# Units 0 to 3 of a sparse attention on two score buffers, ahead of a mixture-style pair of MLPs

## The chip, the cores and the metric

The kernel runs on one core of a Trainium2 chip. The metric is the device time of one execution in microseconds (us): the median of three runs. A profile of one further execution was taken by the hardware profiler, and all rows below come from it.

The engines are named as the profile names them: PE is TensorE (PEld its weight loads), DVE is VectorE, ACT is ScalarE, POOL is GpSimd, and SP is SyncE, which here only issues DMAs. "SPq" is SP's queue of such issues.

## The reference

What is computed is an attention with a sparse mask, then two MLPs on its output:

```python
# q, k, v: batch 4, heads 8, sequence 576, head size 64
scores = scale * q @ k^T          # heads 0-3: local mask, 32 back
scores = where(mask, scores, -1e9)   # heads 4-7: strided mask, every 32nd position
attn = exp(scores - max); attn = attn / (sum(attn) + 1e-9)
x = (attn @ v), laid out as 2304 tokens x 512
gate = sigmoid(x @ w_gate); val = x @ w_val          # 512 -> 1536
x = (gate * val) @ w_out                             # 1536 -> 512
h = x @ w_in; g = softplus(h); return g @ w_out2     # 512 -> 2048 -> 512
```

All in float32. On PE every float32 product of the MLPs is done as three passes with high and low parts (`mm3`, lines 71 to 74: high times high, high times low, low times high), so each weight and each activation exists as a pair, `h` and `l`.

## The kernel before, in words

**Attention.** The 8 heads of a batch are four pairs, and a pair of one batch is a *unit*: 16 units, numbered batch by batch. In each batch the first two units are local (heads 0 to 3) and the last two strided. So units 0 to 3 are batch 0, and their outputs are the first 576 tokens of `x`, each unit one of the four 128-row parts that the MLPs sum over.

A unit goes through these steps, each a function: `load` (q and k by DMA, two transfers) and `load_v` (v, two transfers); `bias` (two matmuls that put the mask into PSUM); `scores` (PE, then on DVE a maximum L1048 and a subtraction L1049 into an SBUF tile `sl` or `ss`); `exponent` (ACT L1056); `normalize` (DVE: a sum L1063 and a reciprocal L1066; POOL: the product L1069); `p_transposes` (PE L1090, then copies `pt` by ACT L1094); `values` (PE L1107 into `ps_o`); `outputs` (ACT writes the high part `xh` L1132, DVE the low part `xl` L1135).

**Weights.** They come as 64-bit words, in pieces of 512 KB (`raw`, three buffers, loaded by `load_next` L104), and are decoded in two steps per piece (`decode_steps`): DVE L122 and L126 give `f`, ACT L150 writes the high half, DVE L132 and L139 give `e`, POOL L152 and L153 write the low half. `f` and `e` have one buffer each during the attention. In the kernel before, L122 and L132 write into a PSUM bank (`ps_x`).

**Order.** Nothing is scheduled by a tool: each engine executes its instructions in the order in which the Python code emits them. `first()` emits units 0 to 3 and the first steps of unit 4, written out by hand, and then yields to the MLP, whose matmuls (`window`, `step`, `gates`) fill PE from there on between the steps of units 4 to 15. All loads are on SP's queue in the order of the code, except k of units 0 and 1, which ACT issues. A load into a tile whose last reader isn't done makes SP wait, and everything behind it on SP.

**Buffers.** PSUM has eight banks: `ps_s` (scores, two banks, one tile), `ps_o` (two banks, one tile), `ps_hy` (three banks; transposes of units 0 to 3, warming matmuls, MLP) and `ps_x` (one, decode). q, k and v have three tiles each; `pt` has one.

**Warming.** `keep_busy(n)` emits n matmuls on constants that nothing reads (`ps_w`, L965): six at the start and single ones in `first()`.

**The gate.** `gates(..., interleave=True)` for the first MLP block alternates the two halves of the gate weights (piece 0 and piece 1) over each part of `x`. The result of both is held back until `release()`.

The lines of `first()` that the prediction speaks of, shortened:

```python
bias(0); scores(0); ...; normalize(0); bias(1); scores(1); load_v(2); load(3)
next(decs[0])                      # L122, L126 of piece 0
p_transposes(0); normalize(1); next(decs[0])
bias(2); scores(2); values(0); load(4); load_v(3); outputs(0)
... values(3); outputs(3); bias(4); scores(4); ...
```

## Time and profile before

| | |
|---|---|
| three runs | 883.06, 885.71, 886.19 us; median 885.71 us |
| the profiled execution | 887.23 us, of which 885.4 us is the span from the first to the last instruction |
| mean granted TensorE clock | 0.992 |
| PE busy | 865.7 us, 98% of the span, 6010 matmuls |
| DVE, POOL, ACT busy | 598.2, 490.2, 420.6 us |
| read from HBM, written | 113.75 MB, 38.27 MB |

The profile's page lists busy time by engine, then the span in 40 slices of 22.1 us each with a digit for the busy tenths, then queues, the chain that ended last, and the costliest groups of instructions. A matmul's end is modelled, so PE's busy time says only that PE had work; the start times are what is measured. An idle stretch is put down to what ended it; "issue" means that no semaphore explains it.

### The profile page before, as it was taken

The page shows a single profiled execution, that of the slowest core. Times are in us where ns is not written, and L with a number is a line of the kernel's source. Part 1 is how long each engine was busy: PE and PEld are TensorE (multiplying, and loading weights), DVE is VectorE, ACT ScalarE, POOL GpSimd, SP SyncE. Part 2 cuts the span into 40 slices and gives each one's busy share as a digit, 9 for nine tenths or more (in the row PEclk, how much of TensorE's full clock was granted, in tenths as well). Part 3 has the DMA queues.
Part 4 walks back from the last instruction along what each step waited for, and adds up shares of the span by engine and source line. Part 5 has one row for each costly group of instructions (what it writes and reads, how often), then busy time and mean ns, then how long its engine had stood idle before and what let it go on. Part 6 is the DMA issues. An engine that isn't in the chain of part 4 may idle for free.

```text
span 885.4 us, 15378 instructions
## 1 busy us (share of the span) xinstructions
PE 865.7 (98%) x6010; PEld 725.0 (82%) x6010; DVE 598.2 (68%) x898; ACT 420.6 (48%) x680; POOL 490.2 (55%) x389
## 2 busy tenths in 40 slices
PE   7799999999999999999999999999999999999998
PEld 5578878888888888888888888888888878888887
DVE  6696776268878888878874645665756574656574
ACT  2366544423333333233333466666667575665641
POOL 5373321037888687788778625466536963343630
PEclk9699999999999999999999999999999999999999
DMA  9696460034675577566644245566575565545403
GB/s 276 179 247 163 122 161 4 1 105 134 241 257 191 190 254 233 180 214 231 223 164 165 72 145 181 192 198 196 195 233 183 192 219 183 187 148 182 151 1 118
DMA packets 61367, 153.01 MB, mean 173 GB/s; under 512 B 6160, under 2 KB 6672, under 8 KB 61296
## 3 DMA queue, kind: packets, MB, share of 16 engines
q1 hardware_dynamic: 61008, 151.42, 53.3%
q8 instruction: 47, 0.77, 0.4%
q10 hardware_dynamic: 288, 0.62, 0.2%
q14 instruction: 24, 0.20, 0.1%
HBM read 113.75 MB, written 38.27 MB: 172 GB/s over the span
## 4 chain that ended last, share of the span: by engine, by line
PE 68%; DVE 4%; ACT 3%; POOL 3%; issue 1%; DVEq 0%; POOLq 0%; ACTq 0%
PE ps_y L72 9%; PE ps_y L73 9%; PE ps_y L74 9%; PE ps_v L72 4%; PE ps_v L74 4%; PE ps_v L73 4%; PE ps_g L72 4%; PE ps_g L74 4%; PE ps_g L73 4%; PE ps_h L74 3%; PE ps_h L73 3%; PE ps_h L72 3%; PE ps_b L72 2%; PE ps_b L73 2%; PE ps_b L74 2%
## 5 line engine op out<-in xcount | busy, mean ns | idle before, releaser
L330 POOL TENSOR_TENSOR b<-b,b 128x512 f32<-128x512 f32 (+1 forms) x42 | 72.5, 1739 | 91.7 <-DVE gl L330 46.1
L241 ACT ACTIVATE gh<-ps_v 128x512 fp32r<-128x512 f32 (+1 forms) x60 | 33.3, 555 | 131.5 <-DVE ps_v L284 131.5
L304 DVE TENSOR_TENSOR acc<-ps_y,acc 128x512 f32<-128x512 f32 (+1 forms) x100 | 62.2, 634 | 48.0 <-PE ps_y L74 47.6
L333 ACT ACTIVATE gh<-b 128x1024 fp32r<-128x1024 f32 (+1 forms) x63 | 57.8, 917 | 40.7 <-DVE b L713 23.9
L469 DVE TENSOR_TENSOR acc<-ps_y,acc 128x512 f32<-128x512 f32 x66 | 44.8, 686 | 41.7 <-PE ps_y L74 40.7
L330 POOL TENSOR_TENSOR gl<-b,gh 128x1024 fp32r<-128x1024 f32 x20 | 49.2, 2458 | 36.5 <-ACT gh L333 36.5
L242 DVE TENSOR_TENSOR gl<-ps_v,gh 128x512 fp32r<-128x512 f32 (+1 forms) x60 | 38.3, 638 | 37.5 <-ACT gh L241 37.5
L189 POOL TENSOR_TENSOR a<-f,e 128x512 f32<-128x512 f32 x32 | 41.4, 1295 | 39.6 <-DVE e L139 39.6
L177 POOL TENSOR_TENSOR pair<-a,pair 128x512 fp32r<-128x512 f32 x32 | 41.5, 1298 | 31.7 <-ACT pair L176 31.7
L330 DVE TENSOR_TENSOR gl<-b,gh 128x1024 fp32r<-128x1024 f32 (+1 forms) x43 | 48.7, 1134 | 14.5 <-ACT gh L333 14.3
L74 PE MATMUL ps_y<-gh,w02l 128*128 128x512 f32 (+1 forms) x144 | 53.8, 374 | 0.4 <-POOL w02l L153 0.4
L72 PE MATMUL ps_y<-gh,w12h 128*128 128x512 f32 (+1 forms) x144 | 54.1, 376 | 0.1
L73 PE MATMUL ps_y<-gl,w12h 128*128 128x512 f32 (+1 forms) x144 | 53.7, 373 | 0.0
L126 DVE SCALAR_TENSOR_TENSOR f<-raw,ps_x 128x512 uint32<-128x512 uint32 x68 | 46.8, 688 | 9.4 <-POOL w11l L153 2.1
L284 DVE TENSOR_TENSOR ps_v<-ps_v,sg 128x512 f32<-128x512 f32 (+1 forms) x60 | 38.5, 641 | 21.2 <-PE ps_v L74 20.0
L74 PE MATMUL ps_y<-gh,w12l 128*128 128x512 f32 (+1 forms) x140 | 52.2, 373 | 0.2 <-POOL w12l L153 0.2
L72 PE MATMUL ps_y<-gh,w02h 128*128 128x512 f32 (+1 forms) x136 | 51.3, 377 | 0.7 <-ACT acc L302 0.6
L176 ACT ACTIVATE pair<-s 128x512 fp32r<-128x512 f32 x32 | 20.2, 632 | 66.4 <-POOL s L203 51.8
L73 PE MATMUL ps_y<-gl,w02h 128*128 128x512 f32 (+1 forms) x136 | 50.7, 373 | 0.2 <-DVE gl L242 0.2
L139 DVE SCALAR_TENSOR_TENSOR e<-raw,ps_x 128x512 f32<-128x512 uint32 x68 | 46.7, 687 | 2.3
L132 DVE TENSOR_SCALAR ps_x<-f 128x512 uint32<-128x512 uint32 x68 | 46.8, 688 | 0.9
L122 DVE TENSOR_SCALAR ps_x<-raw 128x512 uint32<-128x512 uint32 x68 | 46.6, 685 | 0.0
(340 smaller groups left out, 2803.8 us busy)
## 6 DMA issues: line engine op xcount, KB each, us to landing
raw<-in_w_dram SPq DMA_DIRECT2D x68, 512.0 KB, 4.5
in_s<-pair SPq DMA_DIRECT2D x32, 512.0 KB, 2.9
out_s<-pair SPq DMA_DIRECT2D x32, 512.0 KB, 2.9
xh<-in_s SPq DMA_DIRECT2D x64, 256.0 KB, 2.9
xl<-in_s SPq DMA_DIRECT2D x56, 256.0 KB, 3.7
out_dram<-acc SPq DMA_DIRECT2D x16, 256.0 KB, 3.3
w10h<-out_s SPq DMA_DIRECT2D x6, 512.0 KB
w10l<-out_s SPq DMA_DIRECT2D x6, 512.0 KB, 4.0
```

The costliest lines, as they stand in the source:

```text
L72: nc.tensor.matmul(ps, lhsT=lh, rhs=rh, start=first, stop=False, **kw)
L73: nc.tensor.matmul(ps, lhsT=lh, rhs=rl, start=False, stop=False, **kw)
L74: nc.tensor.matmul(ps, lhsT=ll, rhs=rh, start=False, stop=last, **kw)
L122: nc.vector.tensor_scalar(out=part, in0=high, scalar1=3, scalar2=0x3FFFFFFF, op0=ALU.logical_shift_left, op1=ALU.bitwise_and,)
L126: nc.vector.scalar_tensor_tensor(out=f, in0=high, scalar=0xC0000000, in1=part, op0=ALU.bitwise_and, op1=ALU.bitwise_or,)
L132: nc.vector.tensor_scalar(out=e, in0=f, scalar1=0xFF800000, scalar2=None, op0=ALU.bitwise_and)
L139: nc.vector.scalar_tensor_tensor(out=e.bitcast(F32), in0=low, scalar=2.0 ** -52, in1=x.bitcast(F32), op0=ALU.mult, op1=ALU.mult,)
L177: nc.gpsimd.tensor_tensor(out=l, in0=src, in1=h.bitcast(F32), op=ALU.subtract)
L304: nc.vector.tensor_tensor(out=y, in0=ps[:, 0:n], in1=y, op=ALU.add)
L330: eng.tensor_tensor(out=out, in0=a, in1=b, op=ALU.subtract)
L333: nc.scalar.activation(out=op[0], in_=src, func=AF.Copy)
L469: nc.vector.tensor_tensor(out=y, in0=ps, in1=y, op=ALU.add)
```

## The change

Only the stretch up to the first MLP matmuls is touched, that is `first()` and what it uses.

- **Score buffers.** Units 1 and 3 take a second score tile, `ps_s1`, and transposes and warming matmuls take two banks of a new pool `ps_t`. These four banks are those of `ps_hy` and `ps_x`, which are now opened only before `values(3)`.
- **Decode.** As `ps_x` isn't open yet, pieces 0 and 1 are decoded in place: L122 writes `f` itself and L132 writes `e` itself.
- **Copies of odd units** (`pt` of units 1 and 3) and the v of unit 3 go into the accumulator `acc[1]`, which the MLP doesn't use yet.
- **Order.** All score stages come first, then the transposes and values. Two warming matmuls fewer are emitted.
- **Loads.** q, k and v of units 0 to 3 and both first weight pieces are emitted ahead of everything.
- **Gate.** The first block does piece 0 over all parts of `x`, then piece 1.

```diff
@@ gates
-        if interleave:
-            order = [(c, cc) for cc in range(NCC) for c in range(GC)]
@@ attention
-                "hy": pool("ps_hy", 3, space=PSUM), "x": pool("ps_x", 1, space=PSUM),
+            early = ExitStack()
+            ps_s1, ps_t = (
+                early.enter_context(tc.tile_pool(name=name, bufs=bufs, space=PSUM))
+                for name, bufs in (("ps_s1", 1), ("ps_t", 2))
+            )
@@ load_v
+                if i == NPAIR - 1:
+                    t = acc[1][:, 0:NL[0] * 2 * D].rearrange("p (n h d) -> p n h d", h=2, d=D)
+                else:
+                    t = vp.tile([P, NL[0], 2, D], F32, tag="v", name="vt")
@@ bias
+                home = ps_s1 if i < TURN and i % 2 else ps_s
+                ps = home.tile([P, 2, TB], F32, tag="s", name="ps_s")
@@ p_transposes
+                if i < TURN and i % 2:
+                    pt = acc[1][:, NL[0] * 2 * D:].rearrange("p (h n) -> p h n", h=2)
...
+                    ps = both[:, h] if i >= TURN else ps_t.tile([P, TB], F32, tag="t", name="ps_p")
@@ first
+                early.close()
+                pools["hy"] = pool("ps_hy", 3, space=PSUM)
+                pools["x"] = pool("ps_x", 1, space=PSUM)
                 values(TURN - 1)
-                outputs(TURN - 1)
                 bias(TURN)
                 scores(TURN)
+                outputs(TURN - 1)
```

PE, from the scores of unit 0 to those of unit 3, in the kernel before (`ps_s` are scores, `ps_p` transposes, `ps_o` values, `ps_w` warming; the float32 scores and values appear in the trace as two matmuls each; numbers behind a name tell tiles of one name apart):

```order
L1030 MATMUL ps_s_209<-kt_141,qt_140 32x64 x40
L965 MATMUL ps_w_284<-w12l_77,one_164 128x512
L1011 MATMUL ps_s_291<-m_loc_199,one_164 128x320 x2
L1030 MATMUL ps_s_291<-kt_145,qt_144 32x64 x40
L965 MATMUL ps_w_352<-w12l_77,one_164 128x512 x2
L1090 MATMUL ps_p_356<-one_164,sl0_109 128x128 x3
L1090 MATMUL ps_p_361<-one_164,sl0_109 128x128 x3
L1011 MATMUL ps_s_377<-m_str_280,one_164 128x324 x2
L1030 MATMUL ps_s_377<-kt_154,qt_153 64x54 x24
L1107 MATMUL ps_o_407<-pt_355,vt_148 64x32 x36
L1090 MATMUL ps_p_463<-one_164,sl1_110 128x128 x3
L1090 MATMUL ps_p_468<-one_164,sl1_110 128x128 x3
```

The same place in the changed kernel:

```order
L1043 MATMUL ps_s_220<-kt_141,qt_140 32x64 x40
L1024 MATMUL ps_s_294<-m_loc_210,one_175 128x320 x2
L1043 MATMUL ps_s_294<-kt_145,qt_144 32x64 x40
L977 MATMUL ps_w_340<-w12l_77,one_175 128x512
L1024 MATMUL ps_s_352<-m_str_291,one_175 128x324 x2
L1043 MATMUL ps_s_352<-kt_149,qt_148 64x54 x24
L977 MATMUL ps_w_390<-w12l_77,one_175 128x512
L1024 MATMUL ps_s_392<-m_str_291,one_175 128x324 x2
L1043 MATMUL ps_s_392<-kt_156,qt_155 64x54 x24
L1105 MATMUL ps_p_424<-one_175,sl0_109 128x128 x3
L1105 MATMUL ps_p_429<-one_175,sl0_109 128x128 x3
L1122 MATMUL ps_o_443<-pt_423,vt_152 64x32 x36
```

All four scores now stand ahead of the first transposes and values; before, unit 0's transposes stood ahead of unit 2's scores.

DVE, from the low part of unit 1 to that of unit 3, in the kernel before (the decode of piece 0, L122 to L139, stands ahead of it, among the scores of units 1 and 2):

```order
L1135 TENSOR_TENSOR xl_62<-ps_o_503,xh_61 128x320
L1135 TENSOR_TENSOR xl_62<-ps_o_503,xh_61 128x256
L1063 TENSOR_REDUCE st_500<-ss1_112 128x12
L1066 RECIPROCAL st_500<-st_500 128x12
L122 TENSOR_SCALAR ps_x_560<-raw_344 128x512
L126 SCALAR_TENSOR_TENSOR f_558<-raw_344,ps_x_560 128x512
L1135 TENSOR_TENSOR xl_62<-ps_o_576,xh_61 128x2x18x16
L132 TENSOR_SCALAR ps_x_622<-f_558 128x512
L139 SCALAR_TENSOR_TENSOR e_559<-raw_344,ps_x_622 128x512
L1135 TENSOR_TENSOR xl_62<-ps_o_629,xh_61 128x2x18x16
```

In the changed kernel, from unit 1's low part on (ahead of it the four decode steps of piece 0, which before stood among the scores of units 1 and 2):

```order
L1150 TENSOR_TENSOR xl_62<-ps_o_523,xh_61 128x320
L1150 TENSOR_TENSOR xl_62<-ps_o_523,xh_61 128x256
L122 TENSOR_SCALAR f_567<-raw_167 128x512
L126 SCALAR_TENSOR_TENSOR f_567<-raw_167,f_567 128x512
L1150 TENSOR_TENSOR xl_62<-ps_o_581,xh_61 128x2x18x16
L132 TENSOR_SCALAR e_568<-f_567 128x512
L139 SCALAR_TENSOR_TENSOR e_568<-raw_167,e_568 128x512
L1061 TENSOR_REDUCE st_695<-ps_s_652 128x2x5
L1062 TENSOR_TENSOR sl0_109<-ps_s_652,st_695 128x640
L1150 TENSOR_TENSOR xl_62<-ps_o_627,xh_61 128x2x18x16
```

The L122 of piece 1 now writes `f`, which POOL's L153 of piece 0 still reads; before it wrote `ps_x`. Unit 3's low part moved behind unit 4's scores.

SP, from the loads of unit 4's q and k to unit 5's v, in the kernel before (`vt<-in_vl` is v of a local unit, `in_vs` of a strided one):

```order
L917 DMA qt_444<-in_q_dram 128x576
L918 DMA kt_445<-in_k_dram 128x608
L931 DMA vt_448<-in_vs_dram 54x768 x2
L104 DMA raw_451<-in_w1_dram 128x512
L931 DMA vt_540<-in_vl_dram 64x1280
L931 DMA vt_540<-in_vl_dram 64x1024
L917 DMA qt_543<-in_q_dram 128x576
L918 DMA kt_544<-in_k_dram 128x608
L104 DMA raw_547<-in_w1_dram 128x512
L931 DMA vt_601<-in_vl_dram 64x1280
L931 DMA vt_601<-in_vl_dram 64x1024
```

The same loads in the changed kernel, from the v of unit 3 (now in `acc1`) on:

```order
L936 DMA acc1_64<-in_vs_dram 54x768 x2
L919 DMA qt_343<-in_q_dram 128x576
L920 DMA kt_344<-in_k_dram 128x608
L104 DMA raw_382<-in_w1_dram 128x512
L936 DMA vt_484<-in_vl_dram 64x1280
L936 DMA vt_484<-in_vl_dram 64x1024
L919 DMA qt_487<-in_q_dram 128x576
L920 DMA kt_488<-in_k_dram 128x608
L104 DMA raw_521<-in_w1_dram 128x512
L936 DMA vt_564<-in_vl_dram 64x1280
L936 DMA vt_564<-in_vl_dram 64x1024
```

The v of unit 3 stands ahead of unit 4's q and k and no longer waits for `values(0)`; v of unit 4 waits for `values(0)` instead of `values(1)`, v of unit 5 for `values(1)` instead of `values(2)`.

## Rows read from the trace of the kernel before

**Rows 1.** The page: busy time by engine
```profile
PE 865.7 (98%) x6010; PEld 725.0 (82%) x6010; DVE 598.2 (68%) x898; ACT 420.6 (48%) x680; POOL 490.2 (55%) x389
```
**Rows 2.** Busy time by stretch (start:end, length, engines, clock, DMA share, GB/s)
```profile
0.00:42.10 42.10, 29.93 (x710) 22.46 (x710) 24.96 (x49) 11.70 (x22) 17.54 (x39) 0.84 0.83 239
42.10:885.40 843.30, 835.75 (x5302) 702.54 (x5300) 573.27 (x849) 408.92 (x658) 472.67 (x351) 1.00 0.53 170
14.80:28.45 13.65, 9.34 (x311) 7.52 (x307) 11.39 (x21) 6.06 (x14) 6.75 (x8) 1.00 0.90 261
28.45:36.20 7.75, 3.48 (x110) 2.77 (x110) 1.69 (x3) 1.46 (x3) 2.55 (x2) 0.50 1.00 267
36.20:42.10 5.90, 5.81 (x111) 4.32 (x111) 4.14 (x7) 0.74 (x1) 1.23 (x2) 0.50 0.25 96
```
**Rows 3.** Timeline of PE: start, duration, matmuls; idle time and its releaser in brackets
```profile
16.65 0.34 PE L1030 MATMUL ps_s<-kt,qt 64*64 64x54 f32 x8 [1.20 <-issue]
21.93 0.37 PE L1030 MATMUL ps_s<-kt,qt 64*64 64x54 f32 x9 [1.75 <-issue]
25.30 1.29 PE L1107 MATMUL ps_o<-pt,vt 54*64 54x54 f32 x48 [0.78 <-ACT pt L1094]
30.26 0.90 PE L1011 MATMUL ps_s<-m_loc,one 128*128 128x320 f32 x2
31.09 1.13 PE L1030 MATMUL ps_s<-kt,qt 64*32 64x64 f32 x59
36.19 0.64 PE L1030 MATMUL ps_s<-kt,qt 64*32 64x64 f32 x21 [3.97 <-issue]
36.76 0.79 PE L72 MATMUL ps_g<-xh,w00h 128*128 128x512 f32 x1
38.20 0.63 PE L72 MATMUL ps_g<-xh,w00h 128*128 128x512 f32 x1
42.74 0.47 PE L72 MATMUL ps_g<-xh,w00h 128*128 128x512 f32 x1
43.51 0.40 PE L72 MATMUL ps_g<-xh,w00h 128*128 128x512 f32 x1
```
**Rows 4.** DMA queues: the page; then windows 13.8:14.9 and 33.3:36.2
```profile
q8 instruction: 47, 0.77, 0.4%
...
q8 instruction: 1, 0.02, 7.2%
...
q1 hardware_dynamic: 303, 0.73, 98.8%
q8 instruction: 1, 0.02, 2.8%
```
**Rows 5.** Timeline of SP's queue: when the loads were issued
```profile
14.05 0.33 SPq L918 DMA_DIRECT2D kt<-in_k_dram  x1
18.17 0.66 SPq L931 DMA_DIRECT2D vt<-in_vs_dram  x2
26.19 0.38 SPq L104 DMA_DIRECT2D raw<-in_w_dram  x1
26.66 1.68 SPq L931 DMA_DIRECT2D vt<-in_vl_dram  x2
```
**Rows 6.** Timeline of DVE, ACT and POOL, the steps that the sum uses
```profile
7.56 0.82 DVE L1048 TENSOR_REDUCE st<-ps_s 128x10 f32<-128x640 f32 x1 [2.35 <-PE ps_s L1030]
25.82 0.23 DVE L1066 RECIPROCAL st<-st 128x12 f32<-128x12 f32 x1
26.74 0.69 DVE L126 SCALAR_TENSOR_TENSOR f<-raw,ps_x 128x512 uint32<-128x512 uint32 x1
27.35 0.75 DVE L1135 TENSOR_TENSOR xl<-ps_o,xh 128x576 fp32r<-128x576 f32 x1
29.39 1.27 POOL L152 TENSOR_TENSOR f<-f,w00h 128x512 f32<-128x512 f32 x1 [1.78 <-ACT w00h L150]
30.74 1.28 POOL L153 TENSOR_TENSOR w00l<-f,e 128x512 fp32r<-128x512 f32 x1
```

More of the change, by code (lines that the diff above doesn't have):

```diff
@@ L939, in attention @@
             load(1)
+            load(2)
             load_v(0)
+            load(3)
             load_next()
-            load(2)
             load_v(1)
+            load_v(2)
+            load_next()
+            load_v(3)
             scratch = acc[NBA - 1]
@@ L962, in keep_busy @@
             def keep_busy(n):
-                ps = bank(pools, "y", "ps_w")
+                if "hy" in pools:
+                    ps = bank(pools, "y", "ps_w")
+                else:
+                    ps = ps_t.tile([P, TB], F32, tag="t", name="ps_w")
                 for _ in range(n):
@@ L1080, in p_transposes @@
                 flat = sm.pop(i)[0].rearrange("p s w -> p (s w)")
-                pt = ptp.tile([P, 2, 3 * P], F32, tag="pt", name="pt")
+                if i < TURN and i % 2:
+                    pt = acc[1][:, NL[0] * 2 * D:].rearrange("p (h n) -> p h n", h=2)
+                else:
+                    pt = ptp.tile([P, 2, 3 * P], F32, tag="pt", name="pt")
                 n = 2 * P + HP if loc else 3 * P
-                both = None
                 if i >= TURN:
@@ L1086, in p_transposes @@
                 for h in range(2):
-                    ps = both[:, h] if both is not None else bank(pools, "y", "ps_p")
+                    ps = both[:, h] if i >= TURN else ps_t.tile([P, TB], F32, tag="t", name="ps_p")
                     for j in range(3):
@@ L1092, in p_transposes @@
                         )
-                    if both is None:
+                    if i < TURN:
                         nc.scalar.activation(out=pt[:, h, 0:n], in_=ps[:, 0:n], func=AF.Copy)
-                if both is not None:
+                if i >= TURN:
                     nc.scalar.activation(out=pt[:, :, 0:n], in_=both[:, :, 0:n], func=AF.Copy)
@@ L1164, in first @@
             def first():
-                decs = [decode_steps(pools, refill) for refill in (False, True, True)]
+                decs = [decode_steps(pools) for _ in range(3)]
                 bias(0)
@@ L1169, in first @@
                 masks[False] = table("m_str", P + 2 * LK, SQ, SLOTS_S, strided)
-                exponent(0)
-                keep_busy(1)
-                normalize(0)
                 bias(1)
                 scores(1)
-                load_v(2)
-                load(3)
-                load_next()
-                next(decs[0])
-                exponent(1)
-                keep_busy(2)
-                p_transposes(0)
-                normalize(1)
-                next(decs[0])
+                keep_busy(1)
+                exponent(0)
+                load(4)
+                normalize(0)
                 bias(2)
                 scores(2)
-                values(0)
-                load(4)
-                load_v(3)
                 load_next()
-                outputs(0)
-                exponent(2)
-                normalize(2)
-                p_transposes(1)
+                exponent(1)
+                normalize(1)
+                keep_busy(1)
                 bias(3)
                 scores(3)
-                values(1)
+                exponent(2)
+                p_transposes(0)
+                exponent(3)
+                normalize(2)
+                normalize(3)
+                values(0)
+                outputs(0)
                 load_v(4)
                 load(5)
-                load_next()
+                p_transposes(1)
+                p_transposes(2)
+                next(decs[0])
+                next(decs[0])
+                values(1)
                 outputs(1)
-                exponent(3)
-                normalize(3)
+                load_v(5)
                 next(decs[1])
-                keep_busy(1)
-                p_transposes(2)
+                p_transposes(3)
                 values(2)
-                load_v(5)
+                outputs(2)
                 load(6)
-                outputs(2)
-                p_transposes(3)
                 next(decs[1])
+                early.close()
+                pools["hy"] = pool("ps_hy", 3, space=PSUM)
+                pools["x"] = pool("ps_x", 1, space=PSUM)
                 values(TURN - 1)
-                outputs(TURN - 1)
                 bias(TURN)
                 scores(TURN)
+                outputs(TURN - 1)
                 exponent(TURN)
```

2 lines of the change are left out of this document (removed).

## The prediction

> **What bounds the kernel now.** I read the page first: PE is busy for 865.7 of 885.4 us [rows 1], so a change that adds and removes no MLP work can only touch the 20 us in which PE stands still. The view by stretch says where these are [rows 2]: 12.2 us lie ahead of 42.1 (42.10 less 29.93), only 7.6 in the 843 us after it. The change lies wholly ahead of 42.1. What comes after is PE work without gaps, so each microsecond by which the first MLP matmuls start earlier or later reaches the end nearly whole.
>
> PE's timeline shows three stops that no semaphore explains, "issue": 1.20 us before 16.65, 1.75 before 21.93 and 3.97 before 36.19, the last in the middle of unit 4's scores, 59 of 80 matmuls done [rows 3]. The first MLP matmul follows at 36.76. So the last stop ends last here, not the data, the decode or a PSUM bank.
>
> What it waits for is read from two views. Counting matmuls on PE in order, the first stop comes after 221, the second after 126 more, the third after 252 more, twice 126: a stop sits at a fixed distance in the program. And the queue view has a queue of kind "instruction", q8, with 47 transfers of 0.77 MB, 16 KB each [rows 4]. PE has 6010 matmuls and 6010 weight loads [rows 1], 256 for each transfer, 128 matmuls, or 126 where other instructions stand among them. One such transfer lies in the window from 13.8, ahead of the first stop's end, and one in that from 33.3, ahead of the last's, beside data queues that hold the engines for 98.8% of the window [rows 4]. So I read the stops as PE out of instructions, its next block queued behind data that was issued earlier. The block that ends the stop at 36.19 was asked for when PE entered the block before it, 126 matmuls earlier: in unit 2's values, at about 26.4 [rows 3]. Just ahead of that SP had issued a weight piece (26.19) and just behind it v of unit 5 (26.66) [rows 5].
>
> [...]
>
> **The change part by part.** *Scores first.* DVE works on unit 0's scores from 7.56 [rows 6]. In the changed order it then has twelve steps of 0.82 (four maxima, four subtractions, four sums), 9.9 us, and eight small ones, some 2 us with the gaps; the second score tile and the early q and k leave it no reason to wait. It is through with unit 3 at about 19.5; before, unit 3's reciprocal ended at 26.05 (25.82 plus 0.23) [rows 6]. That is 6 us earlier, the visible gain.
>
> *What is late next.* Behind it on DVE now stand low part 0 (0.75), the four decode steps of piece 0 (4 x 0.69 = 2.8) and low part 1: L139 ends at 23 to 24.5, the later end if values or copies hold it up. Then comes a new wait. L122 of piece 1 writes `f`, which POOL's L152 and L153 of piece 0 still use, 1.27 and 1.28 [rows 6] from the end of L132 or of ACT's copy: until 25 to 27. Behind that L122 on DVE are L126 (together 1.4) and low part 2 (0.75), which frees `ps_o` for unit 3's values: 27 to 29. Values 1.3 to 1.5, bias 0.90, scores 1.4 (1.13 for 59 and the rest) [rows 3] bring unit 4's scores to their end at 31 to 33. Before, without the stop, they would have ended at 31.09 plus 1.4, 32.5. So the 6 us of the score stages are spent on decode steps that move from among the scores to behind them: of the compute path nothing is left, within a microsecond and a half. I take zero.
>
> *The block of instructions.* The matmul count hardly moves: two warming matmuls fewer, so the same block ends after 61 instead of 59 matmuls of unit 4's scores, and is again asked for in unit 2's values, at about 26.5 by the path above. What lies ahead of it differs. v of unit 5 now waits for unit 1's values, not unit 2's, so its 0.59 MB (64 x 1280 and 64 x 1024 words of four bytes) are issued before, not after. At 261 GB/s [rows 2] that is 2.3 us more queue. Against it, the DMA engines were busy for 0.90 of the 13.65 us from 14.80 [rows 2]; with loads issued sooner up to 1.4 us of idle time may fill. Net 0.9 us later: PE goes on at about 37.1. The trace does not show this queue, so bounds: no wait at all would let the MLP start at 32.7, 4.1 us earlier; v of unit 5 and both loads of unit 6 (another 0.63 MB, 2.4 us) ahead, with no idle time filled, make it 4.7 us later. I take 0.9, the row nearest in place being the stop itself.
>
> *The clock.* From 28.45 to 42.1 the granted clock is 0.50, that is 1.2 GHz, after a stretch in which PE was busy for 9.34 of 13.65 us; from 42.1 it is 2.4 GHz, after 5.90 us in which PE was busy for 5.81 [rows 2]. Three gate matmuls start 1.44 us apart at the low level (36.76 to 38.20) and 0.77 at the high one (42.74 to 43.51) [rows 3], so a microsecond at the low level carries 0.53 of work. If the clock rises when it did, 0.9 us cost 0.5; if it rises 0.9 later, 0.9. I take 0.7.
>
> *The rest.* Two fewer warming matmuls, 0.5 each, lie in idle time. The gate order asks for piece 1 later, whose low part was ready at 32.0 (30.74 plus 1.28) [rows 6], well ahead of the MLP: nothing. Low part 3 behind unit 4's scores lies beside ACT's exponent. In-place decode: if DVE does SBUF to SBUF faster or slower than through PSUM, half either way of 8 x 0.69 is 2.8 us at most on a path that has up to 4 us of cover from the fetch. Opening `ps_hy` late waits for copies long done.
>
> Sum: 887.23 (span 885.4 and 1.8 around it) plus 0.7 is 887.9. The median of runs is 885.71, 1.5 below the profiled execution, so 886.4.
>
> **The rivals.** *The block comes early.* If instructions need not queue behind data already issued, or the block is asked for before v of unit 5 goes out, the stop shrinks towards nothing. For it: the first two stops were only 1.20 and 1.75 us long [rows 3]. Against it: the transfer of the long stop started more than 6 us after it was asked for. The MLP then starts up to 4.1 us sooner, worth 2.2 (4.1 x 0.53) if the clock rises at 42.1; if it rises with the MLP, a further 5.3 x 0.47 = 2.5 and the other 1.9 come on top, 6.6. So 879.1 to 883.5, middle 881.3.
> [...] The window at 33.3 speaks against it.
>
> *An earlier block becomes the bound (slower).* The block that ended the stop at 21.93 is asked for at about 13 now, and needed three matmuls short of the end of unit 0's values, at about 18.5. Before, SP issued nothing between 14.05 and 18.17, held by unit 0's values [rows 5], so that queue drained. Now v of unit 3 has its own place and nothing holds SP: piece 0, v of units 1 and 2, piece 1 and v of unit 3, 2.3 MB, 8.8 us at 261 GB/s, lie ahead, and with the 2.9 us from the start of a transfer to PE's going on (33.3 to 36.19) PE gets it at 24.5. It decides from a block later than 21: low part 0 and all the decode behind it then start late, and unit 4's scores end at about 38.5, 2 us after 36.5. With the clock low for one more stretch like 36.20 to 42.10 (5.90 x 0.47 = 2.8) that is +2 to +5, 887.7 to 890.7, middle 889.5.
>
> *The overlap isn't there.* If unit 3's scores still wait on q and k, DVE is through with unit 3 later than 19.5 by up to 4 us, and the fetch covers it: 886, inside the forecast.
>
> **How the numbers follow.** Forecast 0.55 (with the last case), its own range 884 to 888.5; block early 0.23; earlier block 0.22. I call no change what lies within 0.5%, 4.4 us, of 885.71, about what a measurement of this kernel can tell. Faster than 881.3 takes half of the early block and a little for in-place decode on a path I mis-sized: 0.20. Slower than 890.1 takes most of the upper half of the earlier block, the 4.7 us bound and a longer low clock: 0.22. The range goes from 880 to 891.
>
> **What would show it.** Right: unit 3's reciprocal on DVE near 20 us; L122 of piece 1 waiting for POOL's L153; an "issue" stop of 3 us or more in unit 4's scores; the first gate matmul between 35.5 and 38.5; PE full after 42. Wrong: no stop in unit 4's scores and a gate matmul before 34 (early block), a stop of over 3 us inside unit 0's values (earlier block), or new PE gaps after 42.

## The result and the profile after

The changed kernel takes 891.4 us (median of 8 runs, 887.24 to 891.79) against 885.5 (median of 8, 883.06 to 887.8) on the same chip: a ratio of 1.0058, interval 1.0036 to 1.0081. It is slower by 5.9 us: not by the forecast's 0.7 us, and by more than the +2 to +5 of the "earlier block" rival. The profiled execution took 891.55 us, of which 889.8 are its span. The profiled execution before took 887.23, itself 1.75 above its median, so the two profiles show 4.4 of the 5.9 us.

First the view by stretch of the kernel after, in the columns of [rows 2]: up to its first gate matmul, from 46.60 on (5.36 us behind that matmul's start, as 42.10 lies 5.34 behind it before), and the three stretches that were shown of before.

```profile
0.00:41.24 41.24, 24.49 (x619) 18.98 (x619) 19.02 (x41) 11.40 (x21) 16.73 (x37) 0.79 0.96 243
46.60:889.80 843.20, 835.58 (x5300) 702.22 (x5300) 575.56 (x849) 409.01 (x658) 472.90 (x351) 1.00 0.53 170
14.80:28.45 13.65, 9.85 (x224) 7.93 (x219) 8.15 (x18) 6.08 (x14) 6.73 (x8) 0.79 1.00 227
28.45:36.20 7.75, 2.72 (x66) 2.39 (x66) 2.34 (x4) 1.58 (x3) 1.57 (x1) 0.65 1.04 217
36.20:42.10 5.90, 2.86 (x84) 2.08 (x83) 0.76 (x1) 0.24 (x1) 1.38 (x2) 0.50 0.78 205
```

And the same view of the kernel before, up to its own first gate matmul (which starts at 36.76 [rows 3]):

```profile
0.00:36.76 36.76, 24.68 (x621) 18.53 (x621) 20.82 (x42) 10.96 (x21) 16.31 (x37) 0.89 0.93 264
```

The long second stretch is the same in both, 843.2 us with PE busy for 835.6, against 843.3 and 835.75 [rows 2]. So the whole loss of these two executions lies ahead of the MLP: the first gate matmul comes 4.48 us later (41.24 less 36.76), as much as the span grew (889.8 less 885.4 is 4.4). Up to it PE does the same work, 24.49 us against 24.68. It stands idle for 16.75 us in place of 12.08. The next view says on what: PE's timeline after, idle time and its releaser in brackets.

```profile
12.19 0.40 PE L977 MATMUL ps_w<-w12l,one 128*128 128x512 f32 x1 [1.11 <-issue]
13.89 1.54 PE L1043 MATMUL ps_s<-kt,qt 64*64 64x54 f32 x48 [1.00 <-DMA kt<-in_k_dram]
20.68 0.42 PE L1122 MATMUL ps_o<-pt,vt 64*64 64x32 f32 x3 [2.02 <-issue]
27.07 0.69 PE L1122 MATMUL ps_o<-pt,vt 54*64 54x54 f32 x32 [0.91 <-PE ps_p L1105]
31.92 0.69 PE L1122 MATMUL ps_o<-pt,vt 54*64 54x54 f32 x16 [4.16 <-issue]
34.18 1.54 PE L1122 MATMUL ps_o<-acc 54*64 54x54 f32 x48 [1.56 <-DVE xl L1150]
36.48 1.15 PE L1043 MATMUL ps_s<-kt,qt 64*32 64x64 f32 x61
40.67 0.64 PE L1043 MATMUL ps_s<-kt,qt 64*32 64x64 f32 x19 [3.04 <-issue]
41.24 0.79 PE L72 MATMUL ps_g<-xh,w00h 128*128 128x512 f32 x1
```

Read the "issue" brackets against [rows 3]. Three stops of 6.9 us have become four of 10.3 (1.11, 2.02, 4.16 and 3.04). The last has not grown: 3.04 in place of 3.97, after 61 of 80 matmuls as counted. The largest is new and stands one block earlier, after 32 of 48 matmuls of unit 2's values, where the kernel before crossed a block border without a stop. The other 1.3 us of idle time are the waits on DVE's xl, on k of unit 3 and on PE's own transposes, less waits on ACT, on POOL and on the mask that have shrunk or gone.

DVE's timeline after shows that the compute path did what was worked out, until the stops:

```profile
18.93 0.23 DVE L1079 RECIPROCAL st<-st 128x12 f32<-128x12 f32 x1
22.63 0.42 DVE L122 TENSOR_SCALAR f<-raw 128x512 uint32<-128x512 uint32 x1
27.85 0.43 DVE L122 TENSOR_SCALAR f<-raw 128x512 uint32<-128x512 uint32 x1 [0.88 <-POOL w00l L153]
33.36 0.76 DVE L1150 TENSOR_TENSOR xl<-ps_o,xh 128x576 fp32r<-128x576 f32 x1 [4.36 <-ACT xh L1147]
```

Unit 3's reciprocal ends at 19.16, 6.9 us earlier than before [rows 6]. L122 of piece 1 waits on L153, as forecast. Then xl of unit 2 stands still for 4.36 us behind ACT's copy, which stands behind the values that PE could not finish at 27.76: it is the stop handed on.

SP's queue after, which answers to [rows 5]:

```profile
12.62 1.43 SPq L936 DMA_DIRECT2D acc<-in_vs_dram  x2
16.97 0.35 SPq L919 DMA_DIRECT2D qt<-in_q_dram  x1
19.61 0.33 SPq L104 DMA_DIRECT2D raw<-in_w_dram  x1
21.14 1.12 SPq L936 DMA_DIRECT2D vt<-in_vl_dram  x2
25.41 1.47 SPq L936 DMA_DIRECT2D vt<-in_vl_dram  x2
```

v of unit 3 is issued at 12.62 (before: 18.17) and v of unit 4 at 21.14 (before: 23.47). PE entered the block ahead of the 4.16 us stop at 20.68. The queue view from 29.0 to 30.5 has the one fetch that ended it, beside data (packets, MB, share of 16 engines):

```profile
q1 hardware_dynamic: 96, 0.27, 101.2%
q8 instruction: 1, 0.02, 5.6%
```

So that block was read from 29.2 us on, 8.6 us after PE had entered the one before it, beside a data queue that held the engines full. That such transfers are what PE waits for shows in the two traces, before and after: each of their seven "issue" stops of 1 us or more in the first 60 us ends 1.3 to 1.6 us after one transfer of the instruction queue has ended (this one at 30.59, PE goes on at 31.92). The fourteen timelines of this case have 37 such stops there. The data moved more slowly, too: 227 and 217 GB/s at a DMA share of 1.00 and more, against 261 and 267 [rows 2].

### The profile page after: what moved, and what is told of

It reads as the page before. It is cut to its first block, busy times and chain, and to the rows that moved or that the text cites. A ratio compares the mean times of both kernels' runs of the same rounds, so it can differ in the third digit from the quotient of the medians.

```text
span 889.8 us, 15373 instructions
## 1 busy us (share of the span) xinstructions
PE 864.9 (97%) x6008; PEld 724.7 (81%) x6008; DVE 599.4 (67%) x898; ACT 421.2 (47%) x680; POOL 490.9 (55%) x389
## 4 chain that ended last, share of the span: by engine, by line
PE 71%; DVE 3%; ACT 1%; POOL 1%; issue 1%; DMA 0%; DVEq 0%; POOLq 0%; ACTq 0%; SPq 0%
PE ps_y L72 10%; PE ps_y L73 10%; PE ps_y L74 10%; PE ps_v L73 4%; PE ps_v L72 4%; PE ps_v L74 4%; PE ps_h L73 4%; PE ps_h L72 4%; PE ps_h L74 4%; PE ps_g L73 4%; PE ps_g L72 4%; PE ps_g L74 4%; PE ps_b L72 2%; PE ps_b L73 2%; PE ps_b L74 2%
## 5 line engine op out<-in xcount | busy, mean ns | idle before, releaser
L241 ACT ACTIVATE gh<-ps_v 128x512 fp32r<-128x512 f32 (+1 forms) x60 | 33.3, 556 | 131.4 <-DVE ps_v L282 131.4
L126 DVE SCALAR_TENSOR_TENSOR f<-raw,ps_x 128x512 uint32<-128x512 uint32 x66 | 45.4, 688 | 9.3 <-POOL w11l L153 2.1
L139 DVE SCALAR_TENSOR_TENSOR e<-raw,ps_x 128x512 f32<-128x512 uint32 x66 | 45.3, 687 | 2.3
L132 DVE TENSOR_SCALAR ps_x<-f 128x512 uint32<-128x512 uint32 x66 | 45.4, 688 | 0.9
L72 PE MATMUL ps_g<-xh,w00h 128*128 128x512 f32 (+1 forms) x120 | 45.3, 377 | 0.0
```

The lines of the kernel that those rows point to most:

```text
L72: nc.tensor.matmul(ps, lhsT=lh, rhs=rh, start=first, stop=False, **kw)
L126: nc.vector.scalar_tensor_tensor(out=f, in0=high, scalar=0xC0000000, in1=part, op0=ALU.bitwise_and, op1=ALU.bitwise_or,)
L132: nc.vector.tensor_scalar(out=e, in0=f, scalar1=0xFF800000, scalar2=None, op0=ALU.bitwise_and)
L139: nc.vector.scalar_tensor_tensor(out=e.bitcast(F32), in0=low, scalar=2.0 ** -52, in1=x.bitcast(F32), op0=ALU.mult, op1=ALU.mult,)
```

## The experiments

All were timed in turn with the kernel before, whose medians over 23 to 35 runs lay between 885.0 and 886.0 us. A ratio is that of the medians, with its interval. Single executions of one kernel lie 2 to 9 us apart, and where two kernels are alike up to a place their profiles can differ there (2 and 7 below). So one profile shows a mechanism, and only the ratio shows a time.

**1. Fewer data ahead of the last block, kernel before.** Its third weight piece, v of unit 5 and the loads of unit 6 go behind unit 4's scores.

```diff
                 load(5)
-                load_next()
                 outputs(1)
...
-                load_v(5)
-                load(6)
                 outputs(2)
...
                 scores(TURN)
+                load_next()
+                load_v(5)
+                load(6)
```

> The kernel before, with one weight piece, v of unit 5 and q, k of unit 6 emitted behind unit 4's scores instead of among units 1 and 2. Theory (instruction blocks queue behind data already issued): the 3.97 us stop in unit 4's scores shrinks to under 1.5 us, the first gate matmul comes at 33 to 34.5 instead of 36.76, and the time falls by 1.5 to 4 us, to 882 to 884. Rival (the stop is something else, the order of compute sets the end): the stop stays at 3 to 4 us and the time stays within 1 us of before.

Measured: 885.78, ratio 1.0000 (0.9989 to 1.0010). PE's timeline:

```profile
31.09 1.34 PE L1030 MATMUL ps_s<-kt,qt 64*32 64x64 f32 x80
32.36 0.50 PE L72 MATMUL ps_g<-xh,w00h 128*128 128x512 f32 x1
37.27 0.44 PE L1090 MATMUL ps_p<-one,sl 128*128 128x128 f32 x2 [1.44 <-POOL sl L1069]
41.13 2.14 PE L1107 MATMUL ps_o<-pt,vt 64*64 64x32 f32 x67 [0.19 <-issue]
```

The stop of 3.97 us is gone: the trace shows all 80 matmuls of the scores in one row, and the first gate matmul starts at 32.36 at a granted clock of 1.00, 4.4 us earlier. So the block had waited behind data, as theory had it. The time did not follow: it is the rival's. PE then waited for POOL's normalisation of unit 4, and unit 4's values ran for 2.14 us at the low clock (0.50); of 4.4 us 1.3 were left at the last matmul of this execution, and none in the median.

**2. The same for the changed kernel,** with the first decode's refill dropped.

```diff
-                decs = [decode_steps(pools) for _ in range(3)]
+                decs = [decode_steps(pools, refill) for refill in (False, True, True)]
...
-                load_v(5)
                 next(decs[1])
...
-                load(6)
                 next(decs[1])
...
                 scores(TURN)
+                load_next()
+                load_v(5)
+                load(6)
```

> The changed kernel, with the third refill, v of unit 5 and q, k of unit 6 emitted behind unit 4's scores. Theory (queue of data ahead of the instruction blocks): the stop in unit 2's values (4.16 us) hardly moves, as what lies ahead of it was issued earlier, but the stop in unit 4's scores (3.04 us) goes; first gate matmul at 37.5 to 39, time 887 to 889.5. Rival (the new order of compute with its in-place decode is the cost): both stops may move, but the first gate matmul stays past 40 and the time at 890 to 892.

Measured: 888.44 (885.12 to 889.16), ratio 1.0024 (1.0011 to 1.0037). The profile is of an execution of 885.12: stops of 1.48 and 1.41 us, none in unit 2's values or unit 4's scores. That is the fastest of the 12, and its first gate matmul comes at 34.72, ahead of the 37.5 to 39 expected. By the medians half of the loss comes back, as theory had it; v of units 3 and 4 are still early here, and experiment 7, with the same loads ahead of unit 4's scores, shows what can stand in an execution of 887.26.

**3. The loads alone.** The kernel before with its own order of computing, and the loads issued as the changed kernel does (v of unit 3 in the accumulator bank).

```diff
...
             load(0)
             load(1)
+            load(2)
             load_v(0)
+            load(3)
             load_next()
-            load(2)
             load_v(1)
+            load_v(2)
+            load_next()
+            load_v(3)
...
```

> The kernel before in its own order of compute, with only the loads of the changed kernel: q, k, v of units 0 to 3 and two weight pieces up front, v of unit 3 in the accumulator. Theory (queue of data): longer stops, 8 to 11 us in all against 6.9, first gate matmul at 39 to 41, time 888 to 891. Rival (order of compute): stops as before, time 885 to 886.5.

Measured: 889.31, ratio 1.0038 (1.0024 to 1.0053). PE's timeline, two of its four stops:

```profile
30.42 0.67 PE L1114 MATMUL ps_o<-pt,vt 54*64 54x54 f32 x11 [3.99 <-issue]
40.38 0.64 PE L1037 MATMUL ps_s<-kt,qt 64*32 64x64 f32 x21 [3.81 <-issue]
```

The new stop in unit 2's values appears at 3.99 us, with nothing of the new order of computing in the kernel. It is the loads that make it. The four stops (1.66 and 1.18 are the other two) sum to 10.6 us, and the ratio is two thirds of the changed kernel's excess; the two intervals overlap.

**4. The block borders moved.** Six warming matmuls of 512 columns become 48 of 64, so that every border comes 42 matmuls earlier in the work.

```diff
-                for _ in range(n):
+                for _ in range(n if n < 6 else 0):
                     nc.tensor.matmul(ps, lhsT=one, rhs=idle, start=True, stop=True)
+                for _ in range(48 if n == 6 else 0):
+                    nc.tensor.matmul(
+                        ps[0:LQ, 0:LK], lhsT=one[:, 0:LQ], rhs=idle[:, 0:LK], start=True, stop=True
+                    )
```

> The kernel before, with the six warming matmuls of 512 columns at the start replaced by 48 of 64 columns and 32 rows out: 42 more instruction pairs in about the same time, no load moved. Theory (a stop sits at a fixed count of instructions and its block is asked for one block earlier): all borders fall 42 matmuls earlier in the work; the third block is asked for at the end of unit 1's values (about 24) rather than in unit 2's, ahead of the weight piece of 26.19, so the stop in unit 4's scores, now after 17 of its 80 matmuls, is under 1 us; first gate matmul at 33 to 34.5, time 881.5 to 884.5. Rival (stops belong to the data or the place in the work): a stop of about 4 us stays in the same place, after about 59 matmuls of unit 4's scores, time 885 to 886.5.

Measured: 886.55, ratio 1.0014 (1.0003 to 1.0025).

```profile
21.64 0.48 PE L1094 MATMUL ps_p<-one,sl 128*128 128x128 f32 x1 [3.64 <-issue]
41.28 0.43 PE L1034 MATMUL ps_s<-kt,qt 64*32 64x64 f32 x25 [1.56 <-issue]
```

The stops moved with the count, to unit 1's transposes and unit 5's scores, and unit 4's scores have none. The places are those of the theory, so a stop belongs to a border and not to what PE does there. The time was missed, and so was the first gate matmul (36.02, not 33 to 34.5): the stop was traded for others.

**5. The order alone.** The changed kernel with v of units 3, 4 and 5 behind the values of units 0, 1 and 2, in the common buffer, about where the kernel before issues them.

```diff
...
             load_next()
-            load_v(3)
...
                 outputs(0)
-                load_v(4)
+                load_v(3)
                 load(5)
...
                 outputs(1)
-                load_v(5)
+                load_v(4)
...
                 outputs(2)
+                load_v(5)
                 load(6)
```

> The changed kernel with its order of work unchanged and only three loads moved: v of unit 3 into the common buffer behind unit 0's values, v of unit 4 behind unit 1's, v of unit 5 behind unit 2's, each about where the kernel before issues it. It computes the same. Theory (the loss is TensorE's instruction blocks, which wait on q8 behind data issued earlier): with three strided loads of 0.59 MB later, the stop of 4.16 us in unit 2's values falls to under 2.5 us, since v of unit 4 no longer stands ahead of that block in a row with v of unit 3; the stops (issue) of the prefix sum to 6 to 8.5 us in place of 10.3; time 886 to 889. Rival A (the new order of computing is dearer by itself: the fifth score buffer's release by the copies, and DVE's xl and xl2 which end 1.6 us late): the stops shrink but waits on DVE, ACT or POOL take their place, and the time stays at 890 to 892. Rival B (what counts is the sum of bytes that is issued before unit 4's scores, wherever they stand): stops stay at about 10 us, moved to another block, 890 to 892.

Measured: 886.3, ratio 1.0003 (0.9990 to 1.0015), an interval that lies wholly under that of the changed kernel.

```profile
21.92 0.42 PE L1118 MATMUL ps_o<-pt,vt 64*64 64x32 f32 x3 [2.50 <-issue]
29.55 0.45 PE L1118 MATMUL ps_o<-pt,vt 54*64 54x54 f32 x16 [0.43 <-issue]
35.18 0.63 PE L1039 MATMUL ps_s<-kt,qt 64*32 64x64 f32 x19 [0.79 <-issue]
```

Theory held: the stop of 4.16 us is 0.43, the last 0.79, and the stops sum to 5.2 us (with one of 1.48), under the 6 to 8.5 expected. (Of the three loads only v of units 4 and 5 have 0.59 MB; that of unit 3, strided, has 0.33.) Rivals A and B fall. The new order of computing, with both gate pieces decoded early, costs and gains nothing that can be measured.

**6 and 7. More gate work behind unit 4's scores,** 15 gate matmuls in place of 6, in the kernels of experiments 1 and 2.

```diff
                 next(decs[2])
                 yield
                 next(decs[2])
                 yield
+                for _ in range(3):
+                    yield
...
-            ahead = 2
-            first_fill = (5, 5, 4, 8)
+            ahead = 5
+            first_fill = (4, 4, 3, 8)
```

> The kernel before with refill 3, v of unit 5 and the loads of unit 6 held back behind unit 4's scores, as in the experiment with the held loads, and in addition 15 gate matmuls (five filler steps) in place of 6 between unit 4's scores and its transposes, taken from the filler steps behind them. It computes the same. Theory (the 4.4 us that the early block gave were given back because TensorE then waited 1.7 us on POOL's normalisation of unit 4, and ran on at the low clock again from about 39 to 46 us): the waits of ps_p on sl fall under 0.3 us and the granted clock holds 2.4 GHz from about 33 us on, so that the time is 881.5 to 884. Rival A (the clock falls whatever is done, since small matmuls of units 5 and 6 follow): the wait goes but the clock is low again from 39 to 46 us, time 884 to 885.5. Rival B (the loads held back are what is late next: k, q or v of unit 6, or a weight piece): a stop on DMA of over 1 us between 40 and 60 us, time 885.5 to 888.

Measured: 884.91, ratio 0.9992 (0.9974 to 1.0010). No wait of PE on POOL for unit 4 is left, and the clock is low (0.50) only from 33.2 to 36.6. In that execution, though, a stop came back in unit 4's scores:

```profile
33.30 0.64 PE L1030 MATMUL ps_s<-kt,qt 64*32 64x64 f32 x21 [2.41 <-issue]
```

It has the lowest median of all, 6.5 us under the changed kernel, but from the kernel before it can't be told apart, and the 881.5 to 884 of the theory were not reached.

> The changed kernel with the first decode's refill dropped and v of unit 5, the loads of unit 6 and one refill held back behind unit 4's scores (as in the experiment before), and in addition 15 gate matmuls in place of 6 between unit 4's scores and its transposes. It computes the same. Theory: against the held version without the fill (888.4) the POOL wait of 1.7 us and the low clock go, 2 to 4 us, so 884.5 to 886.5; it stays behind the kernel before with the same two edits, since the loads up front still hold the block in unit 0's values. Rival (the clock's loss was the early, not the late part: the new order leaves TensorE at the low clock until 35 us): no more than 1 us is gained, 887.4 to 889.

Measured: 888.28, ratio 1.0022 (1.0009 to 1.0034), the same as without the fill (1.0024): the rival's time. Its reason, the low clock, is not the whole: the profile has the stop that the profile of experiment 2 lacked.

```profile
31.07 0.69 PE L1122 MATMUL ps_o<-pt,vt 54*64 54x54 f32 x16 [4.17 <-issue]
```

Of the loads that the change moved forward, v of unit 5 and those of unit 6 come later here; v of units 3 and 4 are left to stand ahead of it.

Experiments 2 and 7 are the same code up to unit 4's scores, and so they also show how near the order of a load and a block can be. PE enters the block ahead of that border, and SP issues v of unit 4, in experiment 2 and then in 7 at these times:

```profile
20.61 0.42 PE L1122 MATMUL ps_o<-pt,vt 64*64 64x32 f32 x3 [1.41 <-issue]
21.06 1.12 SPq L936 DMA_DIRECT2D vt<-in_vl_dram  x2
```

```profile
19.83 0.42 PE L1122 MATMUL ps_o<-pt,vt 64*64 64x32 f32 x3 [2.91 <-issue]
20.28 1.12 SPq L936 DMA_DIRECT2D vt<-in_vl_dram  x2
```

Both times the load goes out 0.45 us behind PE's entry, and in the changed kernel 0.46 (21.14 after 20.68). Yet the block is read from 25.9 on in 2, 5.3 us after the entry and in time, and from 28.4 on in 7, 8.6 us after it. So one code has executions with this stop and without it. That may be why six of the changed kernel's eight runs took 890.5 to 891.8 us and two 887.2 to 887.7; only one of them was profiled, so this is not shown.

**8. More data on purpose.** The kernel before, with v of unit 4 loaded a second time into an idle bank.

```diff
...
                 load_v(4)
+                load_v(4, acc[1][:, 0:NL[0] * 2 * D].rearrange("p (n h d) -> p n h d", h=2, d=D))
                 load(5)
```

> The kernel before with v of unit 4 loaded twice: the second copy goes, in the same shape (0.59 MB on 128 partitions), into an accumulator bank that is idle until the MoE part, right behind the first; nobody reads it. It computes the same. Theory (a block of instructions on q8 waits until the data issued ahead of it are through): at the 261 to 267 GB/s of this stretch 0.59 MB more takes 2.2 us, so the stop in unit 4's scores grows from 3.97 us to 5.5 to 6.5 us (or as much is split between it and the stop or wait ahead of it), the first gate matmul starts at 38.5 to 39.5 us in place of 36.8, and the time is 887.5 to 888.5. Rival A (the block is served in turn with the data and its lateness is a delay of its own): the stop stays at 3.5 to 4.5 us and the time at 885.5 to 886.5. Rival B (what delays it is not the bytes, but that some DMA engines are behind others by the 54-row loads of the strided v): an evenly spread copy adds under 1 us to the stop.

Measured: 887.48, ratio 1.0018 (1.0004 to 1.0031): at the lower edge of the theory's time, and by another way. PE, then SP, then DMA from SP's first load of v of unit 4 to the reading of the block (the view by stretch):

```profile
32.38 0.42 PE L1033 MATMUL ps_s<-kt,qt 64*32 64x64 f32 x21 [0.38 <-issue]
43.14 1.59 PE L1110 MATMUL ps_o<-pt,vt 64*64 64x32 f32 x67 [2.54 <-issue]
```

```profile
25.71 1.24 SPq L933 DMA_DIRECT2D acc<-in_vl_dram  x2
28.62 1.34 SPq L933 DMA_DIRECT2D vt<-in_vl_dram  x2
30.02 1.27 SPq L917 DMA_DIRECT2D qt<-in_q_dram  x1
```

```profile
24.54:29.74 5.20, 3.64 (x63) 2.51 (x63) 4.78 (x9) 3.66 (x9) 1.42 (x2) 1.00 0.79 174
```

The stop in unit 4's scores did not grow by 2.2 us but shrank to 0.38. The copy took SP's time, and v of unit 5 went out at 28.62 in place of 26.66 [rows 5], 2 us later, and the block was read from 29.7 on, most likely ahead of it; the next border had the stop. So it is not enough to ask how much is loaded: when it is issued counts. It also suggests that in the kernel before v of unit 5 stood ahead of this block already. But the block did not wait for all that was issued ahead of it, as the theory has it. PE entered the block before it at about 27.2. By then SP had issued v of unit 4, the copy and q of unit 5, 1.5 MB, from 24.54 on; by 29.74 at most 0.9 MB of that had moved (174 GB/s over 5.2 us). This block passed some 0.6 MB, an estimate; how far one can pass, and when, stays open.

**9. v of unit 3 early, v of units 4 and 5 back** behind unit 1's and unit 2's values.

```diff
                 outputs(0)
-                load_v(4)
                 load(5)
...
                 outputs(1)
-                load_v(5)
+                load_v(4)
...
                 outputs(2)
+                load_v(5)
                 load(6)
```

> The changed kernel with only v of units 4 and 5 moved back, behind unit 1's and unit 2's values; v of unit 3 stays up front in its accumulator bank. It computes the same. It stands between the changed kernel (891.4) and the one with v of unit 3 moved back as well (886.3). Theory: the large stop of the changed kernel (4.16 us in unit 2's values) is the block that stood behind v of unit 4, so it falls to under 1.5 us here, as does the one in unit 4's scores; what is left is the 2 us of unit 0's values, which v of unit 3 delays; time 886 to 888. Rival A (v of unit 3 up front is what costs, since everything behind it is later): the stops of unit 0's values and the next stay at 5 us or more together, time 889 to 891. Rival B: the moved loads are late for their own use, a wait of ps_o on DMA vt, time over 888.

Measured: 887.26, ratio 1.0015 (1.0001 to 1.0029).

```profile
30.46 1.54 PE L1122 MATMUL ps_o<-acc 54*64 54x54 f32 x48 [1.55 <-DVE xl L1150]
35.63 0.63 PE L1043 MATMUL ps_s<-kt,qt 64*32 64x64 f32 x19 [1.72 <-issue]
```

Theory held for unit 2's values, which have no stop, and for the time; the last stop kept 1.72 us (under 1.5 was expected). With experiments 5 and 7 it says which load it most likely was: with v of unit 5 held and v of unit 4 early (7) a stop of 4.17 us stands in unit 2's values, with both later (9) there is none. So v of unit 4 can make the stop of 4.16 us, though not in every execution (2), and v of unit 3 makes at most a small part of the loss. No run moved v of unit 4 alone.

**10. All together for the changed kernel:** experiment 5, with the held loads and the fill of 7.

> The changed kernel with all that the other runs found of use: v of units 3 and 4 behind the values of units 0 and 1, v of unit 5, the loads of unit 6 and one refill behind unit 4's scores, no refill behind the first decode, and 15 gate matmuls in place of 6 between unit 4's scores and its transposes. It computes the same. Theory: the stops of the prefix sum to 3 to 5 us, the first gate matmul starts at 33 to 35 us, the chain of unit 4 is covered, so the time is 882.5 to 885, under both kernels. Rival A (as with the held loads without the move of v: a stop of 4 us stays in some runs in unit 2's values): 886 to 889. Rival B (the gain is given back by the clock: low over most of the prefix, as in the other runs of the new order): stops as in the theory, but the time 885 to 886.5.

Measured: 886.88, ratio 1.0018 (1.0004 to 1.0031). It is under the changed kernel but not under the kernel before; the time is that of rival A, without its stop of 4 us. The stops summed to 5.4 us, about as in experiment 5 (5.2), not 3 to 5, and the first gate matmul started at 35.85, not 33 to 35.

**11. v of unit 4 held back too, kernel before** (experiment 6, and `load_v(4)` behind `scores(TURN)`).

> The kernel before with the held loads and 15 gate matmuls behind unit 4's scores, and v of unit 4 held back behind those scores as well. It computes the same. In the profiled run of the version without this last edit a stop of 2.41 us stood in unit 4's scores; its block landed at 30.9 us, behind v of unit 4 and q and k of unit 5. Theory: with 0.59 MB less ahead of it the block lands about 2.2 us sooner, the stop in unit 4's scores falls under 0.5 us, the first gate matmul starts at 31 to 32.5 us, and the time is 882.5 to 884.5, under the kernel before by 1.5 to 3 us. Rival A (v of unit 4 is late next): a wait of ps_o on DMA vt in unit 4's values of over 1 us, 885 to 887. Rival B (a gain in the first 35 us is given back by a lower clock behind it, as with the first version of the held loads): no stop in unit 4's scores, the clock low for some 7 us between 35 and 50 us, 884.5 to 886.

Measured: 886.45, ratio 1.0010 (0.9995 to 1.0025), not the 882.5 to 884.5 of the theory. The profile is of the slowest execution, 889.82.

```profile
28.93 0.44 PE L1107 MATMUL ps_o<-pt,vt 54*64 54x54 f32 x11 [1.76 <-issue]
34.55 0.64 PE L1030 MATMUL ps_s<-kt,qt 64*32 64x64 f32 x21 [0.16 <-issue]
```

The stop in unit 4's scores went, as expected, and one in unit 2's values came, where the kernel before has none: SP had been held at v of unit 4 until 23.5, and without that wait it issued q and k of unit 5 and a weight piece from 20.46 on. This is the changed kernel's fault in small. The first gate matmul came at 35.12, not 31 to 32.5, and one more stop, of 2.47 us, ends at 50.18.

**12. The wait on xl filled,** the kernel of experiment 9 with four idle matmuls.

```diff
                 values(2)
+                keep_busy(4)
                 outputs(2)
```

> The changed kernel with v of units 4 and 5 moved back, as in the experiment before (887.3), and four idle matmuls of 512 columns (0.39 to 0.43 us each) between unit 2's and unit 3's values, where TensorE waits 1.55 us on DVE's xl. It computes the same. In that experiment the granted clock was 1.2 GHz from 23 to 50 us. Theory (in the new order the clock is what is left of the loss, since idle time in a stretch of small matmuls lowers it): with the wait filled the clock is back at 2.4 GHz before the gate matmuls, from 36 us at the latest, and the time is 884.5 to 886. Rival A (single fills change nothing in the clock): low until 45 to 50 us, 887 to 888. Rival B (four more instructions move the block borders by four matmuls, or the fill outlasts the wait): 0.5 to 1 us more, 887.5 to 888.5.

Measured: 886.74, ratio 1.0019 (1.0003 to 1.0034).

```profile
28.92 1.20 PE L977 MATMUL ps_w<-w12l,one 128*128 128x512 f32 x4
30.54 0.92 PE L1122 MATMUL ps_o<-acc 54*64 54x54 f32 x48 [0.43 <-DVE xl L1150]
35.79 0.65 PE L1043 MATMUL ps_s<-kt,qt 64*32 64x64 f32 x23 [3.12 <-issue]
```

The wait was filled and unit 3's values ran at a granted clock of 1.00 (0.92 us in place of 1.54), but PE then waited 3.12 us at the border, and the gate matmuls behind it ran at 0.50 once more (low from 35.6 to 39.1). The time is not the theory's 884.5 to 886, and from experiment 9 (887.26) it can't be told apart: the theory found no support. I had also misread experiment 9: its clock was low from 11.7 to 39.0, not from 23 to 50.

## Why the prediction was wrong

*What bounds the kernel* was right. The loss is made of instruction blocks that wait behind data: runs that moved only loads took stops away (1, 5, 9) or brought them (3), and one that changed only the count of instructions (4) moved them. No trace shows when a block is asked for, only when its read starts. In the trace before, past 60 us, 38 reads start between 4.7 us before and 3.0 us after PE's entry into the block before (256 PE instructions each, counted from the stops), so taking the entry as the asking is an estimate. Against the block-early rival, that a fetch need not queue behind data already issued, speak the 8.6 us from 20.68 to 29.2; experiment 8, where a block passed some 0.6 MB, speaks for it in part.

*The compute path* was right to a microsecond. I had unit 3's reciprocal at 19.5 (19.16), L122 of piece 1 behind L153 at 25 to 27 (27.85), unit 3's values at 27 to 29 and unit 4's scores done at 31 to 33. Take the stops of 2.02 and 4.16 us out of 34.18, and these and 3.04 out of 41.31, where the scores end, and you have 28.0 and 32.1, an estimate. Experiment 5 gives the same as a time: ratio 1.0003.

*In-place decode* turned out 0.25 us shorter for each of L122 and L132 (0.42 to 0.43 after, 0.67 to 0.69 before), 1.0 us on four, within the bound of 2.8 and on no path that counts.

*The block of instructions* is the step that failed, in two terms. First, the forecast put its whole price on the last block, +0.9 for v of unit 5. That stop got shorter, 3.04 for 3.97: by experiments 1 and 8 v of unit 5 had most likely been ahead of it before too. I had read "asked for at about 26.4" and "issued at 26.66" as an order in time that 0.3 us can't carry. Second, and larger, the block that ends in unit 2's values had no term at all. Between the block of unit 0's values, which the rival priced, and that of unit 4's scores, which the forecast priced, there is one more 126 matmuls on; the kernel before crossed it without a stop, and I took that for a property of the place. It was one of the timing, and a close one: in the kernel before the block was read from 23.24 to 24.61, so by the 1.3 to 1.6 us that the seven stops show from there PE could have gone on at 25.9 to 26.2, an estimate, and it crossed the border at about 26.2. v of unit 4 had been held until 23.47. Released at 21.14, with q and k of unit 5 right behind it, it most likely cost the 4.16 us (9: with v of units 4 and 5 later, no stop there).

*The rival* had the mechanism and the sign: SP, no longer held by a v, runs ahead and fills the queue before an early block is asked for. Its place was half right. In unit 0's values PE went on at 20.68, a stop of 2.02 and not at 24.5; under the 21 from which it was to decide. Its price of +2 to +5 us holds the 4.4 of the two spans only because the larger stop came one block later; that is luck. 891.4 lies 0.7 above the 890.7 it gave, and 0.4 above the end of the range; as a ratio on the 885.71 that I started from it is 890.85, just inside. That the range reached so far is luck too: it did so for a late block in unit 0's values and a longer wait at the last block, and the largest stop came between them. (Two sums there are off by little: 13 plus 8.8 plus 2.9 is 24.7, not 24.5, and the middle of 887.7 to 890.7 is 889.2, not 889.5. Neither bears on this.)

*The clock* was priced as a shift of the low stretch. (The profile gives the granted clock as a share of full speed, and no run shows it in GHz: what the recorded texts call 1.2 and 2.4 GHz are its 0.50 and 1.00.) The low stretch did come later (1.00 from about 44.4 after, 42.1 before), yet PE's busy time up to the first gate matmul is equal, so it added next to nothing there. Where the MLP did start early (1), part of the gain went into another low stretch.

Left open: why the data moved at 227 in place of 261 GB/s at a fuller queue (in 3 it was 232 in the same stretch, so it goes with the loads), what decides whether a block passes data issued ahead of it, and how much of the spread between single executions comes from that. None of these was tried by itself.

## What to carry to other kernels

Here a load that waited for a buffer also held back everything issued behind it (SP issued nothing between 14.05 and 18.17 [rows 5]), and that may be what let an instruction fetch through. Before you give a load its own buffer so that it can go early, list every instruction-block border on the busiest engine and see what will be queued when each block is asked for, those with no stop today as well: the one that cost most here had been crossed with 0.3 us to spare at most, by the estimate above. Time won ahead of a long full stretch counts only if the next chain of small steps and the clock let it through: 4.4 us of earlier start were worth nothing in one run.

## What the runs showed of the hardware

- PE can stand still for instructions where loads are bunched: 1.1 to 4.2 us each in the changed kernel, 10.3 us in all ahead of its first gate matmul. The read of a block can start 1.3 us after PE has entered the one before it (before, 23.24 after 21.93) or 8.6 us after (29.24 after 20.68). In the MLP part, from 42.1 us of the kernel before on, where 42 of the 47 blocks were read, PE stood idle for 7.6 us in 843, for whatever reason.
- DVE's L122 and L132 on 128 x 512 words took 0.42 us from SBUF to SBUF and 0.67 from SBUF to PSUM; L126 and L139, with a second operand, 0.69 either way.
- More DMA busy time with fewer bytes: 227 GB/s at a share of 1.00, 261 at 0.90, in the same 13.65 us of two kernels that load the same in another order.
